# A pre-norm transformer block on one core: queries, keys and values of tiles 4 to 15 in three 512-column chains, logits kept in PSUM

## The chip, the core and the metric

The kernel runs on one core of one Trainium2 chip. The core has a matrix engine (TensorE; in the profile PE, and PEld for its weight loads), a vector engine (VectorE, DVE), a scalar engine (ScalarE, ACT), a general engine (GpSimd, POOL), and SyncE (SP), from which nearly all transfers are issued. Each engine takes its own instructions strictly in order and waits on semaphores for the others. [...] The metric is device microseconds from the first to the last instruction of one execution, as a median of runs.

## The reference: what is computed

x is 2048 rows of 512. The first half of the block is attention, the second a wide layer with a squared ReLU:

```
h   = x + attention(layernorm(x) @ wqkv) @ wo          # 32 heads of 16
out = h + (relu(layernorm(h) @ w1 + b1)**2) @ w2 + b2   # 512 -> 1792 -> 512
```

Attention is local and dilated: row s looks at the eight rows s, s-2, ..., s-14 (those below 0 are masked), with a softmax over these eight for each head. All is float32 in and out.

## The kernel before, in words

The rows are cut into 16 tiles of 128. A tile takes every eighth row or so (`x_v`), so that the eight keys of a query lie in the same partition. All large products are made to float32 accuracy from two parts of each operand, a rounded high part (`hi`, L116, a cast on ACT) and the rest (`lo`, L119, a subtraction on DVE or POOL); `mm3` (L181) sums high by high, low by high and high by low over four blocks of 128, so a product is a chain of 12 matmuls into one PSUM bank.

**Queries, keys, values.** `qkv(t, gp)` makes, for tile t and one of four pairs of head groups `gp`, 128 columns each of queries, keys and values: a chain of 12 matmuls of 384 columns. Tiles 0 to 3 are done pair by pair (16 slots), tiles 4 to 15 in six phases (`first_phase(t0)`) of two tiles and eight chains. ACT copies a chain's bank to the tile `y2` (`evac`, L425), which has two buffers of two chains each; SP stores a full buffer to a DRAM scratch `qkv_d` (`store`, L411), from which SP loads the shifted windows of keys and values (L200) and the queries (L213). `store_halo` (L405) copies a few rows inside that scratch, once for each `gp`.

**Attention** runs on DVE beside the matmuls, as a stream of 32 items of two tiles' worth of one pair `gp`. An item multiplies queries by keys (L276, twice), reduces to logits `lg` (L302, L316), adds the mask (L321, half of the items), takes the maximum (L329), subtracts it (L331); ACT takes the exponential into a PSUM tile `ex` (L335); DVE sums (L298), inverts (L305), scales (L311) and weighs the values (L287, twice); POOL adds the weighed values up to `o` (L346). `lg` lies in SBUF, `ex` in PSUM.

**The order of the work** is written out by a small planner. The program is cut into slots, one to a chain or so; `at(d, ...)` and `after(d, ...)` put a chore at the end of a slot, `after` behind the attention that `pump` adds. `pump` adds attention steps as long as a planned VectorE time (the numbers after `yield`, times `SLOW`) is below the planned TensorE time (the argument of `end_slot`). The numbers only set the order; nothing waits for a clock. The chores of a phase: statistics and normalisation of the next two tiles (`x_stats` on DVE and POOL, `x_norm` on ACT, L151), their transposes (`x_T`, L156, then `hi_T` on ACT and `lo_T` on DVE), loads of their rows (`load_x`, L375), and `weight_job`: load a piece of wo or w1 (L463) into a buffer called `raw`, and five slots later split it into its parts on ACT and POOL.

**The wide layer** takes eight groups s of two tiles. For each of 14 blocks f of the hidden layer, `mlp1` (12 matmuls of 256 columns into one of two banks `mm`), then on ACT relu, square and rounding (`hidden`, L540, L541, L116), POOL's low part `rl`, and three slots later `mlp2` (6 matmuls of 512). During s = 0 the weights w2 are loaded (`load_w2`, L686) three blocks ahead and split on ACT and DVE (`split_w2`). In the same slots the attention output of the next group is transposed (`o_T`), multiplied by wo (`wo_product`) and normalised (`h_norm`). The last two groups are done together as a wide group (512 columns in `mlp1`); `add_b2` (L500, POOL) adds a bias to h, `finish` (L570) adds the result and stores it. One pool of 15 row-sized buffers (`ROWS`) serves xt, xh, xl, raw, h and others in turn.

## Time and profile before

| | |
|---|---|
| median of 3 runs | 528.54 us (527.89 to 528.81) |
| the profiled execution's own time | 529.14 us |
| its span, first to last instruction | 527.3 us |
| TensorE (PE) busy | 519.3 us, 98% |
| weight loads (PEld) busy | 471.3 us, 89% |
| VectorE (DVE) busy | 381.1 us, 72% |
| GpSimd (POOL) busy | 309.9 us, 59% |
| ScalarE (ACT) busy | 251.5 us, 48% |
| granted TensorE clock | 0.998 of full speed |

The profile gives each instruction's start and length, and for an idle stretch of an engine who ended it. Matmuls overlap in the records (a matmul's row is longer than the time to the next one's start), so the cost of a matmul in a stream is read from the starts of the rows, not from its own length. A row "A <- B: total, times, longest" says that A stood idle until B was done.

### The profile page before, as it was taken

The numbers are of one execution on the slowest core, as the hardware profiler recorded it, in microseconds if no ns is written. First come the engines' busy times: TensorE is split into PE (matmuls) and PEld (weight loads), VectorE is DVE, ScalarE is ACT, GpSimd is POOL, SyncE is SP. The second block draws the span as 40 slices with busy tenths as digits, with TensorE's granted clock in tenths as the row PEclk, the third lists the DMA queues.
The fourth block names the chain that finished last, engine by engine and source line by source line (L and its number), as shares of the span: only waits on it lengthen the run. The fifth ranks groups of instructions, "written<-read, shape, count | busy, mean of one in ns | idle before, by whom it ended". The sixth has DMA issues, their size and how long they took to land.

```text
span 527.3 us, 8630 instructions
## 1 busy us (share of the span) xinstructions
PE 519.3 (98%) x3024; PEld 471.3 (89%) x3024; DVE 381.1 (72%) x566; ACT 251.5 (48%) x565; POOL 309.9 (59%) x424
## 2 busy tenths in 40 slices
PE   8999999999999999999999999999999999999997
PEld 7999899999999889988989898898989888888885
DVE  5478999988898799997998899699979324111112
ACT  4623554454347566555626464463636335442421
POOL 4715678778675479686877786776879717000000
PEclk9999999999999999999999999999999999999999
DMA  9568978897678454544544453454435000100002
GB/s 266 175 206 197 277 256 244 254 285 238 183 213 284 132 167 121 173 122 133 180 136 122 131 176 117 133 180 124 126 100 179 8 1 1 40 1 0 2 0 80
DMA packets 70659, 75.93 MB, mean 144 GB/s; under 512 B 6744, under 2 KB 47704, under 8 KB 70616
## 3 DMA queue, kind: packets, MB, share of 16 engines
q1 hardware_dynamic: 69816, 75.00, 47.2%
q8 instruction: 23, 0.38, 0.3%
q10 hardware_dynamic: 800, 0.39, 0.3%
q14 instruction: 20, 0.16, 0.1%
HBM read 58.50 MB, written 16.91 MB: 143 GB/s over the span
## 4 chain that ended last, share of the span: by engine, by line
PE 57%; issue 3%; POOL 3%; ACT 0%; DVE 0%; POOLq 0%; DVEq 0%; ACTq 0%
PE mm L181 25%; PE acc L563 25%; PE wo L181 5%; PE tr L156 2%; POOL rl L119 1%; POOL rs L135 1%; POOL h L500 0%; POOL pr L346 0%; DVE pr L287 0%; POOL rs L137 0%; POOL rs L133 0%; ACT hn L151 0%; DVE h L570 0%; ACT r L540 0%; POOL o L346 0%
## 5 line engine op out<-in xcount | busy, mean ns | idle before, releaser
L346 POOL TENSOR_TENSOR pr<-pr 128x512 f32<-128x512 f32 (+1 forms) x128 | 131.3, 1026 | 37.2 <-DVE pr L287 31.9
L540 ACT ACTIVATE r<-mm,b_sb 128x256 f32<-128x256 f32 (+1 forms) x98 | 49.4, 505 | 120.0 <-PE mm L181 110.2
L119 POOL TENSOR_TENSOR rl<-r,rh 128x256 fp32r<-128x256 f32 x84 | 62.4, 747 | 58.1 <-ACT rh L116 58.1
L287 DVE TENSOR_TENSOR pr<-ex,v 128x1024 f32<-128x1024 f32 x64 | 78.0, 1219 | 5.6 <-POOL o L346 3.1
L276 DVE TENSOR_TENSOR pr<-qp,k 128x1024 f32<-128x1024 f32 x64 | 76.0, 1188 | 5.4 <-ACT qp L220 4.8
L181 PE MATMUL mm<-hh,w_h 128*128 128x256 f32 (+1 forms) x392 | 69.8, 300 | 0.0
L181 PE MATMUL mm<-hl,w_h 128*128 128x256 f32 (+1 forms) x392 | 69.0, 298 | 0.0
L181 PE MATMUL mm<-hh,w_l 128*128 128x256 f32 (+1 forms) x392 | 68.9, 298 | 0.0
L181 PEld LDWEIGHTS mm<-hh,w_h 128*128 128x128 f32 x392 | 59.9, 189 | 6.8 <-ACT r L540 0.2
L425 ACT COPY y<-mm 128x384 f32<-128x384 f32 x64 | 30.3, 481 | 63.1 <-PE mm L181 37.5
L181 PEld LDWEIGHTS mm<-hl,w_h 128*128 128x128 f32 x392 | 56.8, 191 | 2.2
L181 PEld LDWEIGHTS mm<-hh,w_l 128*128 128x128 f32 x392 | 56.7, 191 | 2.2
L563 PE MATMUL acc<-w_h,rh 128*128 128x512 f32 x192 | 58.6, 397 | 0.0
L563 PE MATMUL acc<-w_h,rl 128*128 128x512 f32 x192 | 57.6, 391 | 0.3 <-POOL rl L119 0.3
L563 PE MATMUL acc<-w_l,rh 128*128 128x512 f32 x192 | 57.7, 391 | 0.0
L181 PE MATMUL mm<-wq_h,xh 128*128 128x384 f32 x256 | 56.6, 342 | 0.7 <-ACT xh L116 0.7
L181 PE MATMUL mm<-wq_h,xl 128*128 128x384 f32 x256 | 55.1, 336 | 0.5 <-DVE xl L119 0.5
L181 PE MATMUL mm<-wq_l,xh 128*128 128x384 f32 x256 | 55.2, 336 | 0.0
L119 DVE TENSOR_TENSOR rl<-r,rh 128x512 fp32r<-128x512 f32 x14 | 9.7, 692 | 59.8 <-ACT rh L116 59.8
L181 PEld LDWEIGHTS mm<-wq_h,xl 128*128 128x128 f32 x256 | 45.0, 188 | 1.5 <-DVE xl L119 1.1
L181 PEld LDWEIGHTS mm<-wq_h,xh 128*128 128x128 f32 x256 | 44.2, 188 | 1.8 <-ACT xh L116 1.5
L541 ACT ACTIVATE r<-r 128x256 f32<-128x256 f32 (+1 forms) x98 | 44.0, 448 | 3.1
(76 smaller groups left out, 859.4 us busy)
## 6 DMA issues: line engine op xcount, KB each, us to landing
k<-qkv_d SPq DMA_DIRECT2D x48, 288.0 KB, 2.8
v<-qkv_d SPq DMA_DIRECT2D x48, 288.0 KB, 2.7
qkv_d<-y SPq DMA_DIRECT2D x32, 384.0 KB, 4.1
xt<-in_A_x_dram SPq DMA_DIRECT2D x16, 256.0 KB, 4.3
q<-qkv_d SPq DMA_DIRECT2D x32, 128.0 KB, 3.0
h<-in_A_x_dram SPq DMA_DIRECT2D x16, 256.0 KB, 3.8
out_dram<-h SPq DMA_DIRECT2D x16, 256.0 KB, 2.9
raw<-in_B_w_dram SPq DMA_DIRECT2D x16, 224.0 KB, 4.3
```

Source lines behind the costliest of these rows:

```text
L119: eng.tensor_tensor(out=dst, in0=src, in1=h, op=ALU.subtract)
L135: nc.gpsimd.tensor_tensor(out=rs[:, 0:1], in0=rs[:, 1:2], in1=mhalf, op=ALU.pow)
L156: nc.tensor.transpose(tr[:, k, :], src[:, k * P:(k + 1) * P], ident)
L181: nc.tensor.matmul(ps, l(k), r(k), start=(n == 0), stop=(n == 3 * KB - 1))
L276: nc.vector.tensor_tensor(out=pr.rearrange("p i w h d -> p i w (h d)"), in0=qp[:, j].unsqueeze(2).to_broadcast([P, RI, W, GC]), in1=kwin, ...
L287: nc.vector.tensor_tensor(out=p2, in1=vwin, op=ALU.mult, in0=e1[:, :, :, j * GH:(j + 1) * GH].unsqueeze(4).to_broadcast([P, RI, W, GH, DH]))
L346: nc.gpsimd.tensor_tensor(out=dst, in0=p2[:, :, :w], in1=p2[:, :, w:2 * w], op=ALU.add)
L425: nc.scalar.copy(y[:, :, t % RI * GC:(t % RI + 1) * GC], ps[:, :3 * GP].rearrange("p (j c) -> p j c", j=6))
L540: nc.scalar.activation(r, ps, AF.Relu, bias=b1_sb[:, f:f + 1])
L541: nc.scalar.activation(r, r, AF.Square)
L563: nc.tensor.matmul(acc[j], l[:, j * P:(j + 1) * P], w[f], start=(f == 0 and n < len(js)), stop=(f == FB - 1 and n >= len(terms) - len(js)))
```

## The change

What it does:

- **Three chains of 512 for tiles 4 to 15.** `qkv_of(t, c)` makes all 512 columns of queries (c = 0), keys (1) or values (2) of a tile: 3 chains of 12 matmuls a tile in place of 4. The DRAM scratch is laid out by query/key/value first. `y2` grows to eight groups, a store is 512 KB in place of 384 KB, and attention may start on a group of four tiles only when the value chain of its last pair is stored. For tiles 0 to 3 the chains stay, but each store becomes two, one for each half of the pair.
- **Half-chain slots.** In these phases a slot is half a chain: `mm3` calls back after six matmuls, and chores (transposes too) may be put there. The places of chores are the new tables `XT`, `OT`, `WO`, `HT`, `W2`. `weight_job` still splits five slots after its load, which are now half-chain slots.
- **Logits in PSUM.** One PSUM tile `logits` (the old bank `ex`) of two halves holds an item's logits; mask, maximum, subtraction and exponential work in place.
- **Planned times** of slots and attention steps have other values.
- **Last tile by halves.** The last tile's last six matmuls become twelve of 256 columns in two banks; its other ten-odd blocks are added to h earlier; each half is added and stored by itself, one from SP, one from ACT.
- **Smaller moves.** w2 is loaded two blocks ahead in place of three, the low part of its last block lies in `y2`'s place and not in a row buffer, `ROWS` is 14, `h_norm` of the last group comes a slot earlier, and the four last `add_b2` come together at the start of the wide group.

The diff, cut to its core:

```diff
-ROWS = 15
+ROWS = 14
-SLOW = 1.1, 1.05
+SLOW = 1.08, 1.03
+XT = 9, 11
+OT = 7, 8
+WO = 10, 12
+HT = 20, 22
+W2 = 17, 18
-    qkv_d = dram.tile([2, G // 2, 3, 2, CH + PAD, GC], F32, name="qkv_d")
+    qkv_d = dram.tile([2, 3, G, CH + PAD, GC], F32, name="qkv_d")
...
+        logits = psum.tile([P, 2, RI, W, 2, GH], F32, name="ex")
...
-                lg = att.tile([P, RI, W, 2, GH], F32, name="lg")
+                lg = logits[:, n % 2]
...
-                ex[n] = psum.tile([P, RI, W, 2 * GH], F32, name="ex")
-                yield 0.55
-                nc.scalar.activation(ex[n], lf, AF.Exp, scale=DH ** -0.5)
+                ex[n] = lf
+                yield 0.72
+                nc.scalar.activation(lf, lf, AF.Exp, scale=DH ** -0.5)
...
+        if c is None:
+            for j in range(2):
+                nc.sync.dma_start(chain(e, 2 * gp + j, 0, pos,
+                                        [[R * GC, P], [G * CS, 3], [1, RI * GC]]), y[:, :, j])
+        else:
+            nc.sync.dma_start(chain(e, 0, c, pos, [[R * GC, P], [CS, G], [1, RI * GC]]), y)
...
+    def qkv_of(t, c, mid):
+
+        ps = bank()
+        xh, xl = xT[t]
+        cs = slice(c * D, (c + 1) * D)
+        mm3(ps, lambda k: xh[:, k, :], lambda k: xl[:, k, :],
+            lambda k: wq_h[:, k, cs], lambda k: wq_l[:, k, cs], mid, 3 * KB // 2)
+        at(1, evac, t, 0, c, ps)
...
+        def half(m):
+            end_slot(1.37)
+            chores(m)
+
+        for n in range(6):
+            chores(2 * n)
+            qkv_of(t0 + n % 2, n // 2, lambda: half(2 * n + 1))
+            end_slot(1.37)
...
-                if f + 3 < FB:
-                    load_w2(f + 3)
+                if f + 2 < FB:
+                    load_w2(f + 2)
...
-        after(3, h_norm, s, j)
+        after(2 if s == NS - 1 else 3, h_norm, s, j)
...
-    for j in range(RI):
-        after(0, add_b2, s + 1, j)
+    for j in range(LAST * RI):
+        after(0, add_b2, s + j // RI, j % RI)
...
+    def last_tile(s, j, fs):
+
+
+        u, b, e, i0 = where(NS - 1)
+        h = hs.pop((NS - 1, RI - 1))
+        js = slice(j * P, (j + 1) * P)
+        for c, eng in ((slice(0, D // 2), nc.sync), (slice(D // 2, D), nc.scalar)):
+            ps = psum.tile([P, D // 2], F32, name="half", tag="tr", bufs=2)
+            terms = [(f, l, w) for f in fs for l, w in ((0, w2_h), (1, w2_h), (0, w2_l))]
+            for n, (f, l, w) in enumerate(terms):
+                nc.tensor.matmul(ps, hid[s, f][l][:, js], w[f][:, c], start=(n == 0),
+                                 stop=(n == len(terms) - 1))
+            nc.vector.tensor_tensor(out=h[:, c], in0=ps, in1=h[:, c], op=ALU.add)
+            eng.dma_start(out_v[b, e, i0 + RI - 1, :, c], h[:, c])
```

How the order moves, at three places. A name's number is its buffer; a line number is that of its own kernel.

First TensorE, in the phase of tiles 4 and 5 (xh_563 is tile 4 and xh_594 tile 5 before; 567 and 599 after), around the transposes of the next tile, number 6 (xt_512 before, xt_515 after). Before, the fifth and sixth chain, the transposes, the seventh:

```order
L181 MATMUL mm_708<-wq_h_84,xh_563 128x384 x4
L181 MATMUL mm_708<-wq_h_84,xl_564 128x384 x4
L181 MATMUL mm_708<-wq_l_85,xh_563 128x384 x4
L181 MATMUL mm_735<-wq_h_84,xh_594 128x384 x4
L181 MATMUL mm_735<-wq_h_84,xl_595 128x384 x4
L181 MATMUL mm_735<-wq_l_85,xh_594 128x384 x4
L156 MATMUL tr_768<-ident_80,xt_512 128x128 x4
L181 MATMUL mm_775<-wq_h_84,xh_563 128x384 x4
```

and after, the fifth of six chains, with the transposes in its middle:

```order
L185 MATMUL mm_700<-wq_l_85,xh_599 128x512 x4
L185 MATMUL mm_727<-wq_h_84,xh_567 128x512 x4
L185 MATMUL mm_727<-wq_h_84,xl_568 128x512 x2
L160 MATMUL tr_752<-ident_80,xt_515 128x128 x4
L185 MATMUL mm_727<-wq_h_84,xl_568 128x512 x2
L185 MATMUL mm_727<-wq_l_85,xh_567 128x512 x4
L185 MATMUL mm_773<-wq_h_84,xh_599 128x512 x4
```

The transposes stood behind six chains of 384; now they stand behind four and a half of 512.

Second ScalarE in the same phase: copies of chains (mm) to y2, the normalisation of tile 6 (xt_512, now xt_515) and tile 7 (xt_566, now xt_570), a copy of queries (qp) and the split of wo (wo_h). Before:

```order
L425 COPY y2_90<-mm_614 128x6x64
L425 COPY y2_90<-mm_641 128x6x64
L425 COPY y2_90<-mm_665 128x6x64
L425 COPY y2_90<-mm_690 128x6x64
L151 ACTIVATE xt_512<-xt_512,rs_632 128x512
L220 COPY qp_728<-q_611 128x256
L116 CAST wo_h_86<-raw_635 128x512
L425 COPY y2_90<-mm_708 128x6x64
L151 ACTIVATE xt_566<-xt_566,rs_657 128x512
```

and after:

```order
L442 COPY y2_90<-mm_617 128x8x64
L442 COPY y2_90<-mm_647 128x8x64
L120 CAST wo_h_86<-raw_632 128x512
L442 COPY y2_90<-mm_674 128x8x64
L155 ACTIVATE xt_515<-xt_515,rs_629 128x512
L224 COPY qp_713<-q_614 128x256
L155 ACTIVATE xt_570<-xt_570,rs_657 128x512
L120 CAST wo_h_86<-raw_669 128x512
L442 COPY y2_90<-mm_700 128x8x64
```

Four copies stood ahead of the normalisation of tile 6; now three copies and the first split of wo do.

Third SyncE, where the wide layer begins: loads of w2 (raw2, one for each block f), the last stores of y2, windows of keys and values, and rows of x for h. Before, from the load for f = 2 to that for f = 4:

```order
L686 DMA raw2_1931<-in_B_w2_dram 128x512
L200 DMA v_1936<-qkv_d_77 128x576
L411 DMA qkv_d_77<-y2_90 128x6x128
L200 DMA v_1975<-qkv_d_77 128x576
L200 DMA k_2013<-qkv_d_77 128x576
L213 DMA q_2015<-qkv_d_77 128x2x128
L686 DMA raw2_2037<-in_B_w2_dram 128x512
L478 DMA h_2040<-in_A_x_dram 128x512
L411 DMA qkv_d_77<-y2_90 128x6x128
L686 DMA raw2_2058<-in_B_w2_dram 128x512
```

and after, from the load for f = 1 to that for f = 4:

```order
L737 DMA raw2_1730<-in_B_w2_dram 128x512
L425 DMA qkv_d_77<-y2_90 128x8x128
L204 DMA k_1765<-qkv_d_77 128x576
L204 DMA v_1777<-qkv_d_77 128x576
L737 DMA raw2_1828<-in_B_w2_dram 128x512
L507 DMA h_1831<-in_A_x_dram 128x512
L425 DMA qkv_d_77<-y2_90 128x8x128
L204 DMA v_1837<-qkv_d_77 128x576
L737 DMA raw2_1853<-in_B_w2_dram 128x512
L507 DMA h_1861<-in_A_x_dram 128x512
L737 DMA raw2_1879<-in_B_w2_dram 128x512
```

The load for f = 3 (raw2_2037, now raw2_1853) stood ahead of the last store of y2 and of one load of h; now it stands behind that store and a window of values.

More of the change, by code (lines that the diff above doesn't have):

```diff
@@ L156, in transposes @@
             nc.tensor.transpose(tr[:, k, :], src[:, k * P:(k + 1) * P], ident)
-        now["pe"] += 0.45
+        now["pe"] += 0.44
         return tr
@@ L178, in mm3 @@
         for n, (l, r, k) in enumerate(terms):
-            if mid and n == 2 * KB:
+            if mid and n == at_:
                 mid()
@@ L295, in attention @@
                 pr = dots(0)
[L296 removed]
+                yield 1.22
             if old:
@@ L406, in store_halo, with store @@
                               chain(0, g, 2, PAD, [[0, 2], [0, PAD], [1, GC]]))
-    def store(t, gp, y):
+    def store(t, gp, c, y):
         b, r = divmod(t, 8)
         e, i = divmod(r, 4)
-        nc.sync.dma_start(chain(e, 2 * gp, 0, PAD + CH // 2 * b + i,
-                                [[R * GC, P], [CS, 6], [1, RI * GC]]), y)
+        pos = PAD + CH // 2 * b + i
+        if c is None:
[4 more added lines that the diff above has]
+            nc.sync.dma_start(chain(e, 0, c, pos, [[R * GC, P], [CS, G], [1, RI * GC]]), y)
         if t == 0:
@@ L415, in store, with evac @@
         if i == R - RI:
-            stored.add((t // R, gp))
+            if c is None:
+                stored.add((t // R, gp))
+            elif c == 2:
+                stored.update((t // R, gp) for gp in range(G // 2))
     ys = {}
-    y2 = wpool.tile([P, 2, 6, RI * GC], F32, name="y2", tag="y2")
-    def evac(t, gp, ps):
+    y2 = wpool.tile([P, 2, G, RI * GC], F32, name="y2", tag="y2")
+    def evac(t, gp, c, ps):
+        j = 6 if c is None else G
         if t % RI == 0:
-            ys[gp] = y2[:, nbank[0] // RI % 2]
-        y = ys[gp]
+            ys[gp, c] = y2[:, nbank[0] // RI % 2, :j]
+        y = ys[gp, c]
         nc.scalar.copy(y[:, :, t % RI * GC:(t % RI + 1) * GC],
-                       ps[:, :3 * GP].rearrange("p (j c) -> p j c", j=6))
+                       ps[:, :j * GC].rearrange("p (j c) -> p j c", j=j))
         if t % RI == RI - 1:
-            at(0, store, t - t % RI, gp, ys.pop(gp))
+            if c is None:
+                y = y.rearrange("p (c j) n -> p c j n", c=3)
+            at(0, store, t - t % RI, gp, c, y)
+            del ys[gp, c]
+    def qkv_of(t, c, mid):
[5 more added lines that the diff above has]
+        at(1, evac, t, 0, c, ps)
     def qkv(t, gp, mid=None):
@@ L552, in mlp1, with mlp2 @@
         at(1, hidden, s, f, ps)
-    def mlp2(s, f, acc, js):
+    def mlp2(s, f, acc, js, last=FB - 1):
         rh, rl = hid[s, f]
@@ L564, in mlp2 @@
                              start=(f == 0 and n < len(js)),
-                             stop=(f == FB - 1 and n >= len(terms) - len(js)))
+                             stop=(f == last and n >= len(terms) - len(js)))
     def finish(s, j, a):
@@ L650, in block_kernel, with chores @@
             x_T(n - 10)
-        end_slot(1.95)
+        end_slot(2.09)
     def first_phase(t0):
-        for n in range(8):
-            gp, t = n // 2, t0 + n % 2
+        def chores(m):
             if t0 + 3 < 16:
-                if n in (0, 1):
-                    at(0, x_stats, t0 + 2 + n)
-                if n in (4, 5):
-                    at(0, x_norm, t0 - 2 + n)
-                if n in (6, 7):
-                    x_T(t0 - 4 + n)
-            if t0 + 5 < 16 and n in (4, 6):
-                at(0, load_x, t0 + 2 + n // 2)
-            k = 8 * ((t0 - 12) // 2) + n - 4
-            if k in (10, 11):
-                h_T(0, k - 10)
-                after(0, add_b2, 0, k - 10)
-            qkv(t, gp)
-            if jobs and n % WJ == 0:
-                at(0, weight_job)
-            if k in (0, 1):
-                at(0, load_h, 0, k)
-                o_T(0, k)
-            if k in (3, 4):
-                wo_product(0, k - 3)
-                now["pe"] += 2.6
-            if k in (7, 8, 9):
-                at(0, load_w2, k - 7)
-            end_slot(1.95)
+                if m in (0, 2):
+                    at(0, x_stats, t0 + 2 + m // 2)
+                if m in (6, 7):
+                    at(0, x_norm, t0 - 4 + m)
+                if m in XT:
+                    x_T(t0 + 2 + XT.index(m))
+            if t0 + 5 < 16 and m in (6, 9):
+                at(0, load_x, t0 + 2 + m // 3)
+            if jobs and m % 3 == 0:
+                at(0, weight_job)
+            k = t0 // 2 * 12 - 72 + m
+            if k in OT:
+                at(0, load_h, 0, OT.index(k))
+                o_T(0, OT.index(k))
+            if k in WO:
+                wo_product(0, WO.index(k))
+                now["pe"] += 2.73
+            if k in HT:
+                h_T(0, HT.index(k))
+                after(0, add_b2, 0, HT.index(k))
+            if k in W2:
+                at(0, load_w2, W2.index(k))
+        def half(m):
[5 more added lines that the diff above has]
+            end_slot(1.37)
     def load_w2(f):
@@ L693, in block_kernel @@
     big2_l = wpool.tile([P, 12, D], F32R, name="w2_l", tag="big_l")
-    big2_x = wpool.tile([P, 3, D], F32R, name="w2_x", tag="y2")
+    big2_x = wpool.tile([P, 4, D], F32R, name="w2_x", tag="y2")
     for f in range(12):
         w2_h[f], w2_l[f] = big2_h[:, f, :], big2_l[:, f, :]
-    w2_h[12], w2_l[12], w2_h[13] = [big2_x[:, n, :] for n in range(3)]
-    w2_l[13] = row("w2l", dt=F32R)
+    w2_h[12], w2_l[12], w2_h[13], w2_l[13] = [big2_x[:, n, :] for n in range(4)]
     def split_w2(f):
@@ L736, in block_kernel @@
                 mlp2(s, f - LAG, acc, js)
-                more += 1.3
-            end_slot(1.3 + more)
+                more += 1.39
+            end_slot(1.44 + more)
         for n, f in enumerate(range(FB - LAG, FB)):
@@ L759, in block_kernel @@
         if f >= LAGW:
-            mlp2(s, f - LAGW, acc, js)
+            for j in (js[:-1], js[-1:]) if f == FB - 1 else (js,):
+                mlp2(s, f - LAGW, acc, j, FB - 1 if len(j) > 1 else f - LAGW)
         end_slot(5.4 if f >= LAGW else 2.7)
-    for j in js:
+    h = hs[NS - 1, RI - 1]
+    for j in js[:-1]:
         for f in range(FB - LAGW, FB):
@@ L767, in block_kernel @@
         at(0, finish, s + j // RI, j % RI, acc[j])
+        if j == 1:
+            at(0, nc.vector.tensor_tensor, h, acc[-1], h, ALU.add)
         if j:
             run(due)
-    run(due)
+    last_tile(s, js[-1], range(FB - LAGW, FB))
 _INS = ['A_x', 'A_wqkv', 'A_wo', 'B_w1', 'B_b1', 'B_w2', 'B_b2']
```

32 lines of the change are left out of this document (15 added, 17 removed).

## The prediction, made before the changed kernel was run

> **What bounds it.** I read the page's head first, then who waited for whom, then the matrix engine's starts in order of time, then the engines that its waits name.
>
> ```profile
> PE 519.3 (98%) x3024; PEld 471.3 (89%) x3024; DVE 381.1 (72%) x566; ACT 251.5 (48%) x565; POOL 309.9 (59%) x424
> ```
>
> TensorE is busy for 98%, so time goes only with what its stream needs and the few holes in it. What a matmul costs there is read from starts. Rows of 384-column chains (one row is four matmuls, a chain is three rows) and, from the chain of waits, of 256 and 512 columns:
>
> ```profile
> 18.91 0.85 PE L181 MATMUL mm<-wq_h,xh 128*128 128x384 f32 x4
> 35.55 0.85 PE L181 MATMUL mm<-wq_h,xh 128*128 128x384 f32 x4
> ...
> 214.29 1.43 PE mm L181 x12
> 215.72 1.39 PE acc L563 x6
> ...
> 219.92 2.72 PE wo L181 x12
> ```
>
> From 18.91 to 35.55 lie eight chains: 16.64 / 8 = 2.08 us, 173.3 ns a matmul. At 512 columns it is 2.72 / 12 = 226.7 ns, at 256 it is 119 ns. 128 columns more cost 53.4 ns, so about 13 ns of each matmul do not depend on its width.
>
> The holes, with what ended each at the row's end; by starts they are larger, since a row outlasts its matmul:
>
> ```profile
> 44.68 0.95 PE L181 MATMUL mm<-wq_h,xh 128*128 128x384 f32 x4
> 45.84 0.97 PE L181 MATMUL mm<-wq_h,xl 128*128 128x384 f32 x4 [0.21 <-DVE xl L119]
> ...
> 47.37 0.86 PE L181 MATMUL mm<-wq_h,xh 128*128 128x384 f32 x4
> 48.48 0.96 PE L181 MATMUL mm<-wq_h,xl 128*128 128x384 f32 x4 [0.26 <-DVE xl L119]
> ...
> 57.63 0.86 PE L181 MATMUL mm<-wq_l,xh 128*128 128x384 f32 x4
> 59.49 0.66 PE L156 MATMUL tr<-ident,xt 128*128 128x128 f32 x4 [1.01 <-ACT xt L151]
> ...
> 64.61 0.85 PE L181 MATMUL mm<-wq_h,xh 128*128 128x384 f32 x4
> ```
>
> Four matmuls of 384 take 0.69 us. So 0.47, 0.42 and 1.17 us are lost, all in the phase of tiles 4 and 5, which lasts from 44.68 to 64.61. Two more come later, and the end:
>
> ```profile
> 191.08 0.63 PE L563 MATMUL acc<-w_l,rh 128*128 128x512 f32 x2
> 192.00 0.73 PE L563 MATMUL acc<-w_h,rl 128*128 128x512 f32 x2 [0.29 <-POOL rl L119]
> ...
> 444.39 0.62 PE L563 MATMUL acc<-w_x,rl 128*128 128x512 f32 x2
> 445.23 0.65 PE L156 MATMUL tr<-ident,hn 128*128 128x128 f32 x4 [0.21 <-ACT hn L151]
> ...
> 523.53 0.69 DVE h L570
> ```
>
> Two matmuls of 512 take 0.45 us, so these lose 0.47 (0.55 with a slow restart) and 0.39 us. After the last addition, which ends at 524.22, 3.1 us pass to the span's end at 527.3.
>
> **The change part by part**, against the profiled execution's 529.14 us.
>
> *Chains, tiles 6 to 15.* Ten tiles: 40 chains of 2.08 become 30 of 2.72, 83.2 to 81.6: -1.6 us. Nothing hides it either way. Transposes put into a chain's middle are as many as before. A wait could appear here: `weight_job`'s split comes after five half chains, 6.8 us, not five chains, 10.4 us, and stands in ACT's queue ahead of copies. The loads land in 4.3 us (below), so it costs nothing while SP issues them in time.
>
> [...]
>
> *The phase of tiles 4 and 5.* Its pace is set on ACT by the tile-6 normalisation:
>
> ```profile
> 57.87 0.86 ACT L425 COPY y<-mm 128x384 f32<-128x384 f32 x2 [4.71 <-DMA qkv_d<-y]
> 58.62 0.82 ACT L151 ACTIVATE xt<-xt,rs 128x512 f32<-128x512 f32 x1
> ...
> 52.22 1.19 SPq L405 DMA_DIRECT2D qkv_d<-qkv_d  x2
> 53.51 0.35 SPq L463 DMA_DIRECT2D raw<-in_A_wo_dram  x1
> 53.95 0.38 SPq L411 DMA_DIRECT2D qkv_d<-y  x1
> ...
> raw<-in_A_wo_dram SPq DMA_DIRECT2D x4, 256.0 KB, 3.1
> raw<-in_B_w_dram SPq DMA_DIRECT2D x16, 224.0 KB, 4.3
> ...
> L116 ACT CAST xh<-tr 128x512 fp32r<-128x512 f32 x16 | 9.4, 590 | 5.7 <-PE tr L156 5.7
> ```
>
> Before it, ACT copies two chains into a y2 buffer that becomes free when the store issued at 53.95 lands, just before 57.87. That store is late because SP stood behind the halo copies until 52.22. All this stays. Now one copy, of 512 columns (0.59, as the cast of that size), stands between the landing and the normalisation, not two (0.75): -0.16 us. The wo split is new ahead of it, but its load lands at 53.51 + 3.1 = 56.6 and the split ends by 57.3, before the store lands. The store itself is two issues; each of the three stores in question adds up to 0.4 us on SP, so it lands 0 to 1.2 us later. The transfers ahead of the middle one were still moving when it was issued, so I take 0.3. After the transposes come one and a half chains of 512, not two of 384: 4.08 for 4.16. Sum -0.16 + 0.3 - 0.08, so about 0, with -0.3 and +1.0 as ends. The stream reaches the transposes earlier (4.5 chains of 2.72, 12.2 us, stand ahead of them and not 6 of 2.08, 12.5) and waits longer. So the 0.9 us lost on xl go into the longer wait, and the width gains nothing here.
>
> *Logits in PSUM.* Groups of the same size, in SBUF (first three) and in PSUM:
>
> ```profile
> L331 DVE TENSOR_TENSOR lg<-lg,mx 128x128 f32<-128x128 f32 x32 | 20.2, 632 | 1.1
> L329 DVE TENSOR_REDUCE mx<-lg 128x16 f32<-128x128 f32 x32 | 12.4, 388 | 0.0
> L321 DVE TENSOR_TENSOR lg<-lg,mask 128x128 f32<-128x128 f32 x16 | 8.2, 514 | 0.3
> L311 DVE TENSOR_TENSOR ex<-ex,sm 128x128 f32<-128x128 f32 x32 | 9.1, 285 | 0.0
> L298 DVE TENSOR_REDUCE sm<-ex 128x16 f32<-128x128 f32 x32 | 9.0, 281 | 5.4 <-ACT ex L335 5.4
> ...
> 190.00:264.00 74.00, 73.71 (x469) 66.08 (x468) 69.29 (x103) 43.45 (x105) 59.57 (x77) 1.00 0.48 144
> ```
>
> Subtraction and mask should fall to 285 ns, the maximum to 281: 32 x 0.347 + 16 x 0.229 + 32 x 0.107 = 18 us of DVE. The reductions into PSUM have no row; L311 writes PSUM, L298 SBUF, and they differ by 4 ns, so I add nothing. DVE is not on the path: the gain is worth what it saves TensorE in waits. The window from 190 shows DVE busy for 69.29 of 74 us; POOL's rl at 191 stood behind sums that waited for DVE. With DVE ahead I take -0.4 of these 0.55 (ends 0 and -0.55).
>
> [...]
>
> *The start of the wide group.* The normalisation that TensorE awaited at 445.23 came after two bias additions on POOL, now moved behind it:
>
> ```profile
> 441.75 1.25 POOL h L500
> ...
> 444.36 0.83 ACT hn L151
> ```
>
> One addition alone, 1.25 us, exceeds the hole: -0.4 (ends 0 and -0.4). POOL has nothing to do later that the moved additions could delay.
>
> *The end.* Six matmuls of 512 (1.36) become twelve of 256 (1.43), +0.07. The last addition of 128x512 (0.69) becomes 128x256, and that size has a row:
>
> ```profile
> L119 DVE TENSOR_TENSOR hl<-tr,hh 128x256 fp32r<-128x256 f32 x32 | 12.0, 417 | 24.1 <-ACT hh L116 24.1
> q<-qkv_d SPq DMA_DIRECT2D x32, 128.0 KB, 3.0
> ```
>
> -0.27. A transfer of 128 KB lands in 3.0 us, about the 3.1 that pass now with 256 KB, so nothing more: -0.2 (ends -0.7, if half the bytes save half a microsecond, and +0.2, if ACT issues slower).
>
> *w2 two blocks ahead.* At the start of the wide layer ACT waited for w2 even before:
>
> ```profile
> 167.23 0.62 ACT L116 CAST w_h<-raw 128x512 fp32r<-128x512 f32 x1 [1.16 <-DMA raw<-in_B_w_dram]
> 167.75 0.47 ACT L540 ACTIVATE r<-mm,b_sb 128x256 f32<-128x256 f32 x1
> ...
> 169.64 0.64 PE L181 MATMUL mm<-hh,w_h 128*128 128x256 f32 x4
> ```
>
> That is the part for f = 3. Behind the cast stand relu, square and rounding of the block before, without which `mlp1` gets no bank two blocks later. That relu, at 167.75, ended 1.4 us before the bank was needed at 169.64. The load now stands behind the last store of y2 and a window too: two issues of some 0.4 (the store at 53.95), within the 1.4. I take +0.2; 0 at the low end, the high end is a rival.
>
> Sum: -1.6 + 0 - 0.4 - 0.4 - 0.2 + 0.2 = -2.4, 526.7 of 529.14. The median lies 0.60 below the profiled time: 526.1.
>
> **The rivals.**
> *The wait at tile 6 grows.* Three stores in halves are six issues; if all six fall on the path (+1.2) and the wo split, whose load stands behind the halos too, is not hidden (0.64), the phase loses 1.7 where I have 0: -0.7, 527.8, no change. For it: ACT stood 4.71 us for that store. Against: the splits' loads land first.
> *Every hole closes.* If the store lands early, the phase is six chains of 2.72 and eight transposes (0.66 for four at 59.49, of which a third outlasts them; 0.9 in all), 17.2 us, not 19.93: -2.7, and with -1.6, -0.55, -0.4 and -0.5 it is -5.8, 522.8. Against it: nothing moves the halo copies.
> *Width brings nothing.* The six mlp2 matmuls in 1.39 us are 231.7 ns each, and 4/3 of 173.3 is 231: at that price the chains save 0, -0.8 in all, 527.7. Against it: the wo chains, of just this form, at 226.7. [...]
> *w2 comes late: slower.* SP once stood 6.3 us before a load of w2 until a row buffer was free:
>
> ```profile
> SPq L686 <- PE wo L181: 6.3, 1, 6.3
> ```
>
> With one block less of lead and 14 rows, such a hold at f = 2 to 5 makes the cast 6.3 late; beyond 1.4 TensorE waits, 4.9 us. In place of +0.2: -2.4 - 0.2 + 4.9 = +2.3, 530.8. Past 4.0 us of lateness the gain is gone. Against it: the row pool loses one row but also the low part of w2 that sat in it.
>
> **How the numbers follow.** Forecast 0.63; grown wait 0.12; all holes closed 0.08; width without gain 0.05; late w2 0.12. A difference under 0.2% (1.1 us) can't be told from none: below 527.5 is faster. Forecast and closed holes give 0.71 faster, the grown wait and the gainless width 0.17 the same, late w2 0.12 slower. The forecast's own bounds run from -3.4 (every low end) to about 0, 525.1 to 528.5; I take 524.9 to 528.4, which leaves out most of closed holes and late w2.
>
> **What would show it.** Right: q, k and v chains at 2.72 us; one hole left before 64 us, at tile 6's transposes, of some 2 to 2.5 us, ended by ACT xt, and none on xl; maximum and subtraction at some 285 ns; no wait on rl at 191 and none on hn before the wide group; the last addition at 0.42 us. Wrong: a wait of TensorE on a bank or on rl between 160 and 205 us with ACT behind a load of w2; chains at 2.77; reductions into PSUM far over 1.21 us; new waits on xl or xt in later phases.

## The result, and the profile after

The changed kernel takes 523.85 us (median of 4 runs, 523.36 to 524.87) against 528.44 (528.54 in the first three runs): ratio 0.992, 95% interval 0.9907 to 0.9933. The forecast was 526.1, range 524.9 to 528.4: the direction is right, the size is not, about twice the gain forecast. Measured side by side three more times, the changed kernel took 524.38, 523.28 and 523.73 beside 528.63, 528.06 and 528.70.

The profiled execution took 523.98 us, 5.16 less than that of before, with a span of 522.2. The page's line of engines:

```profile
PE 516.7 (99%) x2886; PEld 453.1 (87%) x2886; DVE 373.3 (71%) x568; ACT 250.9 (48%) x553; POOL 310.3 (59%) x424
```

TensorE's starts at the ends of the stages, first of the kernel before (the one such row that is not shown above), then of the changed one; the last three rows are the end:

```profile
158.82 0.63 PE L181 MATMUL mm<-hh,w_h 128*128 128x256 f32 x4
```

```profile
44.84 1.17 PE L185 MATMUL mm<-wq_h,xh 128*128 128x512 f32 x4
...
56.74 0.61 PE L185 MATMUL mm<-wq_h,xl 128*128 128x512 f32 x2
57.62 0.66 PE L160 MATMUL tr<-ident,xt 128*128 128x128 f32 x4 [0.27 <-ACT xt L155]
...
62.70 1.09 PE L185 MATMUL mm<-wq_h,xh 128*128 128x512 f32 x4
...
155.51 0.64 PE L185 MATMUL mm<-hh,w_h 128*128 128x256 f32 x4
...
440.86 0.60 PE L160 MATMUL tr<-ident,hn 128*128 128x128 f32 x4
...
518.80 0.28 PE L613 MATMUL half<-w_x,rh 128*128 128x256 f32 x1
519.12 0.42 DVE L615 TENSOR_TENSOR h<-half,h 128x256 f32<-128x256 f32 x1 [0.29 <-PE half L613]
519.58 0.35 ACTq L616 DMA_DIRECT2D out_dram<-h  x1
```

From start to start, in us:

| stage | before | after | difference | forecast |
|---|---|---|---|---|
| span's start to tile 4 | 44.68 | 44.84 | +0.16 | 0 |
| tiles 4 and 5 | 19.93 | 17.86 | -2.07 | 0 |
| tiles 6 to 15 (with wo) | 94.21 | 92.81 | -1.40 | -1.6 |
| wide layer, to the last transposes of hn | 286.41 | 285.35 | -1.06 | -0.6 (-0.4 -0.4 +0.2) |
| from there to the span's end | 82.09 | 81.32 | -0.77 | -0.2 |
| sum | | | -5.14 | -2.4 |

In these two executions three quarters of the error lie in one stage, tiles 4 and 5. What is left there is one hole, between the rows at 56.74 and 57.62: two matmuls of 512 take 0.45, so 0.43 us are lost. The waits on xl, rl and hn are gone. The -2.07 is made up of -1.0 on xl, -0.74 at tile 6 (1.17 to 0.43) and -0.3 from the chains themselves (eight of 2.08 became six of 2.72). SyncE and ScalarE in that stage:

```profile
50.28 1.24 SPq L412 DMA_DIRECT2D qkv_d<-qkv_d  x2
...
52.52 0.89 SPq L422 DMA_DIRECT2D qkv_d<-y  x2
```

```profile
56.27 0.59 ACT L442 COPY y<-mm 128x512 f32<-128x512 f32 x1 [0.76 <-DMA qkv_d<-y]
56.75 0.82 ACT L155 ACTIVATE xt<-xt,rs 128x512 f32<-128x512 f32 x1
```

The chain is the one that the prediction described (halo copies, store, its landing, copy, normalisation, transposes), but all of it comes 1.4 to 1.9 us earlier: halo copies 50.28 for 52.22, store 52.52 for 53.95, normalisation 56.75 for 58.62. The groups of VectorE:

```profile
L309 DVE TENSOR_REDUCE ex<-pr 128x64 f32<-128x1024 f32 x32 | 39.2, 1226 | 1.0
L338 DVE TENSOR_TENSOR ex<-ex,mx 128x128 f32<-128x128 f32 x32 | 9.6, 300 | 1.1
L336 DVE TENSOR_REDUCE mx<-ex 128x16 f32<-128x128 f32 x32 | 8.9, 278 | 0.0
L328 DVE TENSOR_TENSOR ex<-ex,mask 128x128 f32<-128x128 f32 x16 | 4.7, 295 | 0.3
```

Subtraction 632 to 300 ns, maximum 388 to 278, mask 514 to 295: as forecast. The reductions into PSUM take 1226 ns each, 18 more than into SBUF before (1208).

### The profile page after: what moved, and what is told of

Read it like the earlier page. It is cut to its first block, busy times and chain, and to the rows that moved or that the text cites. A ratio compares the mean times of both kernels' runs of the same rounds, so it can differ in the third digit from the quotient of the medians.

```text
span 522.2 us, 8355 instructions
## 1 busy us (share of the span) xinstructions
PE 516.7 (99%) x2886; PEld 453.1 (87%) x2886; DVE 373.3 (71%) x568; ACT 250.9 (48%) x553; POOL 310.3 (59%) x424
## 4 chain that ended last, share of the span: by engine, by line
PE 96%; DMA 2%; SPq 0%; issue 0%; ACT 0%; DVE 0%; ACTq 0%
PE mm L185 53%; PE acc L592 29%; PE wo L185 8%; PE tr L160 4%; DMA qkv_d<-y 2%; DMA xt<-in_A_x_dram 1%; PE half L613 0%; SPq L412 0%; ACT xh L120 0%; ACT xt L155 0%; DVE st L131 0%; DVE xt L151 0%; DVE h L615 0%; SPq L382 0%; SPq L422 0%
## 5 line engine op out<-in xcount | busy, mean ns | idle before, releaser
L185 PE MATMUL mm<-wq_h,xl 128*128 128x512 f32 (+1 forms) x208 | 55.2, 378 | 0.0
L185 PE MATMUL mm<-wq_h,xh 128*128 128x512 f32 (+1 forms) x208 | 53.2, 377 | 0.7 <-ACT xh L120 0.7
L185 PE MATMUL mm<-wq_l,xh 128*128 128x512 f32 (+1 forms) x208 | 52.7, 375 | 0.0
L442 ACT COPY y<-mm 128x512 f32<-128x512 f32 (+1 forms) x52 | 28.6, 556 | 45.2 <-PE mm L185 24.6
L120 ACT CAST rh<-r 128x256 fp32r<-128x256 f32 (+1 forms) x98 | 43.0, 438 | 3.1
L185 PEld LDWEIGHTS mm<-wq_h,xh 128*128 128x128 f32 x208 | 37.8, 188 | 7.2 <-ACT xh L120 1.8
```

What stands on the lines that cost most here:

```text
L120: nc.scalar.copy(dst, src)
L185: nc.tensor.matmul(ps, l(k), r(k), start=(n == 0), stop=(n == 3 * KB - 1))
L442: nc.scalar.copy(y[:, :, t % RI * GC:(t % RI + 1) * GC], ps[:, :j * GC].rearrange("p (j c) -> p j c", j=j))
```

## Experiments

What is open: why tiles 4 and 5 lost 2 us. The candidates: **H**, halves of the first stores land earlier; **D**, a lighter VectorE; **L**, the new layout of the scratch; **W**, the chains of 512 with the new places of copies and normalisations. Later came **C** and **S**, named below. Runs of one kernel differ by 2 us and more (before: 526.93 to 531.57), so each experiment is read twice: by its median, and by the places in its profile. The table has the second, worked out from the starts of SyncE's, VectorE's and TensorE's rows. "First store": from its issue to the start of the first halo copy, which waits for it (with halves, for the first half alone); "x rows": when VectorE, waiting for a load of x rows, goes on; "halo": start of the last two halo copies; then the time lost on xl in the first chains of tiles 4 and 5, at tile 6's transposes, and the time of tiles 4 to 15 together.

| kernel | first store | x rows | halo | xl | tile 6 | tiles 4-15 | median |
|---|---|---|---|---|---|---|---|
| before | 3.82 | 32.27 | 52.22 | 1.01 | 1.17 | 114.14 | 528.4 |
| halves (b_halves) | 3.08 | 31.55 | 49.62 | 0.11 | 0 | 112.84 | 528.39 |
| PSUM (b_psum) | 3.39 | 31.48 | 50.86 | 0.48 | 0.35 | 112.75 | 527.88 |
| end (b_ends) | 4.17 | 32.62 | 52.21 | 1.45 | 0.81 | 114.20 | 527.99 |
| these three (b_three) | 2.81 | 30.77 | 49.84 | 0 | 0.17 | 112.54 | 526.53 |
| earlier normalisation (b_norm) | 4.01 | 32.25 | 51.80 | 1.05 | 0 | 113.60 | 527.94 |
| halo copies later (b_halo) | 3.55 | 32.20 | moved | 1.08 | 0 | 113.29 | 528.10 |
| changed | 2.92 | 31.15 | 50.28 | 0 | 0.43 | 110.67 | 523.85 |
| again (a_again) | 3.37 | 31.55 | 50.82 | 0 | 1.24 | 111.48 | 524.38 |
| third (a_third) | 3.24 | 30.46 | 49.50 | 0 | 0 | 110.21 | 523.28 |
| fourth (a_fourth) | 3.31 | 30.90 | 49.84 | 0 | <0.1 | 110.26 | 523.73 |
| whole stores (a_whole2) | 3.99 | 32.43 | 51.43 | 0.26 | 0.65 | 111.20 | 524.77 |
| logits in SBUF (a_sbuf) | 3.34 | 31.06 | 50.32 | 0 | 0.69 | 110.94 | 524.83 |
| both of these (a_ws) | 4.28 | 32.28 | 51.51 | 0.11 | 0.91 | 111.36 | 525.20 |
| earlier normalisation (a_norm) | 3.02 | 30.22 | 48.83 | 0 | 0 | 110.19 | 523.31 |
| the same (a_norm_b) | 3.52 | 32.01 | 51.02 | 0 | 0 | 110.46 | 523.39 |
| halo copies later (a_halo) | 3.70 | 31.99 | moved | 0 | 0 | 110.30 | 523.34 |
| both moves (a_both) | 3.35 | 31.05 | moved | 0 | 0 | 110.22 | 523.39 |

What "x rows" decides is the loss on xl. In the kernel before, VectorE stands still until the load of x rows lands and then works without a gap up to the first of the two xl; the same rows of the changed kernel follow:

```profile
32.27 0.69 DVE L127 BATCH_NORM_STATS2 st<-xt 128x6 f32<-128x512 f32 x1 [3.05 <-DMA xt<-in_A_x_dram]
...
45.11 0.68 DVE L119 TENSOR_TENSOR xl<-tr,xh 128x512 fp32r<-128x512 f32 x1
```

```profile
31.15 0.69 DVE L131 BATCH_NORM_STATS2 st<-xt 128x6 f32<-128x512 f32 x1 [2.25 <-DMA xt<-in_A_x_dram]
...
44.15 0.68 DVE L123 TENSOR_TENSOR xl<-tr,xh 128x512 fp32r<-128x512 f32 x1
```

From the one to the other pass 12.8 to 13.0 us in every profile, 12.8 with the logits in SBUF and 13.0 with them in PSUM. So a lighter VectorE does not bring xl earlier here; an earlier load does.

**One part of the change added to the kernel before.** Halves (the changed store for tiles 0 to 3, in the old layout; shortened):

```diff
+        pos = PAD + CH // 2 * b + i
+        if t < R:
+            y = y.rearrange("p (c j) n -> p c j n", c=3)
+            for j in range(2):
+                nc.sync.dma_start(chain(e, 2 * gp + j, 0, pos,
+                                        [[R * GC, P], [2 * CS, 3], [1, RI * GC]]), y[:, :, j])
...
```

> The kernel before, with one thing changed: each store of tiles 0 to 3 is two transfers of 192 KB in place of one of 384 KB. Theory H (the halves land earlier than the whole store, and all that waits for a store moves up): the first halo copy goes from 18.83 to about 18.1 us, the halo copies at 52.22 to about 50.5, the two losses on xl (0.9 us) vanish and the wait at tile 6 shrinks from 1.17 to 0.5-1; 1.4 to 1.9 us faster than before, 526.5 to 527.0. Rival D (it is the lighter VectorE that moved the phase) and rival L (the new layout of the DRAM scratch did): halo copies stay at 18.8 and 52.2, the phase of tiles 4 and 5 at 19.9 us, no change in time, or 0.2 us slower for eight issues more.

Measured 528.39, ratio 1.0002 (0.9991 to 1.0013). In its profile the halo copies come early, and the stage is short; but the loss moves on to tile 7's transposes:

```profile
18.24 1.34 SPq L405 DMA_DIRECT2D qkv_d<-qkv_d  x2
...
49.62 1.24 SPq L405 DMA_DIRECT2D qkv_d<-qkv_d  x2
```

```profile
59.40 0.86 PE L181 MATMUL mm<-wq_l,xh 128*128 128x384 f32 x4
60.45 0.66 PE L156 MATMUL tr<-ident,xt 128*128 128x128 f32 x4 [0.20 <-ACT xt L151]
...
63.03 0.86 PE L181 MATMUL mm<-wq_h,xh 128*128 128x384 f32 x4
63.91 0.96 PE L181 MATMUL mm<-wq_h,xl 128*128 128x384 f32 x4
```

0.36 us are lost at 60.45, because in chains of 384 the next copy stands behind the next store, and 0.2 on an xl at 63.91. The times show no gain from halves alone. The early halo copies came in the old layout, so they do not need the new one (L); no run changes the layout alone. Logits in PSUM, as the change has them (shortened):

```diff
+        logits = psum.tile([P, 2, RI, W, 2, GH], F32, name="ex")
-                lg = att.tile([P, RI, W, 2, GH], F32, name="lg")
+                lg = logits[:, n % 2]
-                ex[n] = psum.tile([P, RI, W, 2 * GH], F32, name="ex")
-                nc.scalar.activation(ex[n], lf, AF.Exp, scale=DH ** -0.5)
+                ex[n] = lf
+                nc.scalar.activation(lf, lf, AF.Exp, scale=DH ** -0.5)
```

> The kernel before with the logits kept in PSUM, planned times as before. Theory H: the phase of tiles 4 and 5 stays at 19.9 us (within 0.3), since the first store is late before attention has begun; only the wait on rl at 191 us (0.55 with its restart) shrinks; 0.3 to 0.6 us faster, about 528.0. Rival D: the halo copies at 52.22 come 1.5 us or more earlier and the phase loses 1 to 2 us; 526 to 527. Subtraction 632, maximum 388 and mask 514 ns all fall to 280-300 in either case.

527.88, ratio 0.9991 (0.9979 to 1.0003). The wait on rl is gone (the wide layer to hn loses 0.50 us of start to start), as H and the forecast had it. The halo copies came 1.4 us earlier too, but the first store landed 0.4 earlier already, before any logit is computed: part of that is the execution's own. The end, with `last_tile` and the `mlp2` calls of the change:

```diff
-        after(3, h_norm, s, j)
+        after(2 if s == NS - 1 else 3, h_norm, s, j)
-                after(0, add_b2, s + 1, f - FB + RI)
-    for j in range(RI):
-        after(0, add_b2, s + 1, j)
+    for j in range(LAST * RI):
+        after(0, add_b2, s + j // RI, j % RI)
-    for j in js:
+    for j in js[:-1]:
...
-    run(due)
+    last_tile(s, js[-1], range(FB - LAGW, FB))
```

> The kernel before with the last tile by halves, the four bias additions together at the start of the wide group and the last normalisation a slot earlier. By the two traces: the hole of 0.39 us before the wide group goes, and from the start of the last matmul to the span's end pass 3.4 us and not 4.26; 1.2 us faster, about 527.2. By the prediction's terms: 0.4 and 0.2, 0.6 us faster, about 527.8.

527.99, ratio 0.9994 (0.9983 to 1.0005). The profile shows the two fixed gains (from the last transposes of hn to the end 81.5 for 82.09 us, and the hole of 0.38 ahead of them gone), 1.0 us together; the interval reaches to -0.9. From the last matmul's start to the span's end pass 3.56 us, not the 3.4 expected. All three together:

> The kernel before with halves of stores, logits in PSUM and the changed end together, and without the chains of 512 and their slots. If the chains are worth the 1.2 us of TensorE that the rows of tiles 6 to 15 show and nothing else, this is 1.2 us slower than the changed kernel, 525.1. By theory W it is 2.2 to 2.8 slower, since the new places in the phase of tiles 4 and 5 are lacking too: 526.1 to 526.7. If the three do not add up beyond what they gave alone (0.04, 0.55 and 0.44 us), 527.4.

526.53, ratio 0.9966 (0.9949 to 0.9983). That lies where W put it, but not for W's reason. Parts of a difference that do not vary between executions (the wide layer up to hn and the stretch behind it agree within 0.02 us in four profiles of the changed kernel) can be read from the stages: against the changed kernel 1.40 us in tiles 6 to 15, 0.3 in tiles 4 and 5 (eight chains of 2.08 for six of 2.72) and 0.3 in the wide layer and the end, 2.0 of the 2.15 by medians. So by medians the two kernels have about the same holes. Against the kernel before, 0.5 (rl) and 1.0 (end) of the 2.10 are fixed and 0.6 are holes.

**One part taken out of the changed kernel.** Whole stores (the scratch then laid out head group first, so that six pieces lie at one stride):

```diff
-        block = (e * 3 + c) * G + g
+        block = (e * G + g) * 3 + c
-            for j in range(2):
-                nc.sync.dma_start(chain(e, 2 * gp + j, 0, pos, ...), y[:, :, j])
+            nc.sync.dma_start(chain(e, 2 * gp, 0, pos, [[R * GC, P], [CS, 6], [1, RI * GC]]), y)
```

> The changed kernel with the stores of tiles 0 to 3 whole again (384 KB each); for that the DRAM scratch is laid out by head group first and query/key/value second, a layout that neither kernel has. Theory H: first halo copies back at 18.8, those of the phase of tiles 4 and 5 at 52 or later; that phase loses 1.5 to 2.3 us at tile 6; 525.4 to 526.2. Rivals D and L: as the changed kernel, 523.9 within 0.4.

525.30 (523.64 to 526.24, 4 runs). Its profile can't be used for the stage: TensorE's first chain began 1.5 us late (9.71 for 8.19), its matmuls then started 320 ns apart until 12.4 us (some 175 in the kernel before), tile 4 began 2.8 us late, and the stores had that much time. So again, with two others:

> The changed kernel with the stores of tiles 0 to 3 whole (and the scratch laid out by head group first), again. Theory H (halves land earlier): 1.0 to 1.6 us slower than the changed kernel. Theory W (the new places of copies, normalisation and stores in the phase of tiles 4 and 5 took the holes away, whatever the size of the stores before it) and theory D (the lighter VectorE did): within 0.3 of it.

Logits back in SBUF:

```diff
-                lg = logits[:, n % 2]
+                lg = att.tile([P, RI, W, 2, GH], F32, name="lg")
-                ex[n] = lf
+                ex[n] = logits[:, n % 2].rearrange("p i w j h -> p i w (j h)")
-                nc.scalar.activation(lf, lf, AF.Exp, scale=DH ** -0.5)
+                nc.scalar.activation(ex[n], lf, AF.Exp, scale=DH ** -0.5)
```

> The changed kernel with the logits back in SBUF (the exponential writes PSUM), planned times as they are. Theory D: the holes of the phase of tiles 4 and 5 come back, 1 to 2 us, and the wait on rl at 190 us too, 0.5: 525.4 to 526.4. Theories H and W: only the wait on rl comes back, and VectorE behind the plan by 18 us may bring others after 120 us: 524.3 to 525.

> The changed kernel once more, beside the three others of this call, since runs of one kernel differ by up to a microsecond or two: 523.9 within 0.3, and in its profile a hole at tile 6 of 0 to 0.8 us, none on xl, rl or hn.

Whole stores 524.77 (ratio 0.9937, 0.9915 to 0.9959), logits in SBUF 524.83 (0.9931, 0.9912 to 0.995), changed 524.38 (0.9916, 0.9898 to 0.9935): no two of them can be told apart. Logits in SBUF bring no hole of 1 to 2 us, so D is out as the main cause, and for xl the 12.8 to 13.0 us above say the same. What logits in SBUF cost is a wait in the wide layer, on another tile than rl:

```profile
203.77 0.83 PE L185 MATMUL mm<-hl,w_h 128*128 128x256 f32 x4 [0.34 <-DVE hl L123]
```

The changed kernel's own hole was 1.24 us this time, ended as ever:

```profile
58.25 0.66 PE L160 MATMUL tr<-ident,xt 128*128 128x128 f32 x4 [1.08 <-ACT xt L155]
```

Both parts out (these two diffs together), against the kernel before with the changed end:

> The changed kernel without two of its parts: stores of tiles 0 to 3 whole, logits in SBUF. Against the kernel before with the changed end alone (528.0) it differs by the chains of 512, their slots and the planned times. If the chains bring the 1.2 us of TensorE and nothing else: 526.8. By theory W (their new places also take 1 us of holes out of the phase of tiles 4 and 5): 525.6 to 526.0. Against the changed kernel: 0.5 for the wait on rl, and 0.4 to 1.0 for whole stores.

> The changed kernel, a third time, to compare the others of this call with: 524.0 within 0.4; a hole at tile 6 of 0.3 to 1.3 us.

525.20 (0.9953, 0.9939 to 0.9967) beside 523.28 (0.9916, 0.9903 to 0.9928), below what either theory gave, since both counted too little as fixed. Its profile speaks for W: the chains with their new places took the losses on xl (1.01 to 0.11) and left 0.91 at tile 6:

```profile
58.24 0.66 PE L160 MATMUL tr<-ident,xt 128*128 128x128 f32 x4 [0.74 <-ACT xt L155]
```

Its median speaks against W: it is 2.86 below that of the kernel before, measured beside it, and the stages' fixed parts make 2.8 of it (1.4, 0.3 and 1.1 behind the chains). Of the 1.92 us to the changed kernel, 0.72 are the wide layer (that much longer to hn in the profile, with the wait on hl), 1.15 are holes in tiles 4 to 15.

**Where the hole at tile 6 comes from.** Theory C: only ScalarE's order carries the store's landing to TensorE. In both kernels the normalisations come two slots earlier (shown for the changed one):

```diff
-                if m in (6, 7):
-                    at(0, x_norm, t0 - 4 + m)
+                if m in (4, 5):
+                    at(0, x_norm, t0 - 2 + m)
```

> The kernel before with the normalisations of the next two tiles two slots earlier, ahead of the third copy to y2. Theory C: the hole at tile 6 (1.17 us in the profile before) goes, the two waits on xl stay; 0.7 to 1.2 us faster than before, 527.3 to 527.8. Rival: within 0.3 of before, because the pace is the stores' own and the wait turns up at the next tile's copy or on a PSUM bank.

> The changed kernel with the normalisations of the next two tiles two half-chain slots earlier, ahead of the third copy to y2 on ScalarE. Theory C (the hole at tile 6 is the landing of the last store of tiles 0 to 3, carried to TensorE only by ScalarE's order: copy first, normalisation behind it): the hole of 0.4 to 1.3 us at tile 6 is gone in the profile and nothing takes its place; 0.4 to 0.8 us faster than the changed kernel, 523.2 to 523.6. Rival: the normalisation waits for its statistics instead, or the casts of xh come late behind the copy: no gain, 524.0 to 524.6.

The kernel before took 527.94 (0.9995, 0.9984 to 1.0005). The hole at tile 6 is gone, since the normalisation now runs at 52.63 and not at 58.62, ahead of the copy that waits for the landing:

```profile
52.63 0.83 ACT L151 ACTIVATE xt<-xt,rs 128x512 f32<-128x512 f32 x1
57.32 0.48 ACT L425 COPY y<-mm 128x384 f32<-128x384 f32 x1 [3.85 <-DMA qkv_d<-y]
```

TensorE and VectorE further on:

```profile
83.29 0.86 PE L181 MATMUL mm<-wq_h,xh 128*128 128x384 f32 x4
84.22 0.97 PE L181 MATMUL mm<-wq_h,xl 128*128 128x384 f32 x4
...
82.40 1.17 DVE L331 TENSOR_TENSOR lg<-lg,mx 128x128 f32<-128x128 f32 x1
83.49 0.68 DVE L119 TENSOR_TENSOR xl<-tr,xh 128x512 fp32r<-128x512 f32 x1
```

The lower rows show a loss in a new place, 0.24 us on the xl of a later tile. No store is in it: VectorE, without a gap, has a subtraction of 1.17 us ahead of that xl. Another 0.2 us are lost on an xl at 64.17. So tiles 4 to 15 take 0.54 us less, not 1.17. C holds for the place, and the forecast of 0.7 to 1.2 us failed. The changed kernel with the same move took 523.31; its sister beside it happened to have no hole either, so this pair says nothing of the gain. Theory S: what makes the store late is SyncE's order. The store issued at 53.95 had its data since the copy that ended at 47.68; it stood behind halo copies that wait for the store before it. They go one slot later, behind that store:

```diff
-            at(2, store_halo, gp)
+            at(3 if gp else 2, store_halo, gp)
```

> The kernel before with the halo copies of head groups 2 to 8 one slot later, so that on SyncE they stand behind the next store of y2 and not ahead of it; nothing else is moved. Theory S (the pace of the phase of tiles 4 and 5 is set by stores that are ready and stand behind halo copies: the one issued at 53.95 had its data at 47.68): that store goes out by 48.5, the hole at tile 6 and the waits on xl go, the phase takes 17.7 to 18.0 us and not 19.93; 1.5 to 2.2 us faster than before, 526.3 to 526.9. Rival: the landing itself is the limit (the queue is full), the store goes earlier and lands as late; within 0.5 of before.

> The changed kernel with the same move of the halo copies. Theory S: no hole at tile 6 whatever the chip; 523.2 to 523.4 with a spread of 0.3, as its runs without a hole had. Rival: as the changed kernel beside it.

> The changed kernel with the normalisations two half-chain slots earlier, again. Where the changed kernel beside it has a hole at tile 6, this one has none: 523.2 to 523.5, and a spread of 0.3.

> The changed kernel, to compare the others with: between 523.2 (no hole) and 524.5 (a hole of 1.2 us at tile 6).

The kernel before, SyncE, ScalarE and TensorE:

```profile
48.13 0.44 SPq L411 DMA_DIRECT2D qkv_d<-y  x1
51.62 1.19 SPq L405 DMA_DIRECT2D qkv_d<-qkv_d  x2
```

```profile
54.72 0.81 ACT L151 ACTIVATE xt<-xt,rs 128x512 f32<-128x512 f32 x1
```

```profile
45.77 0.97 PE L181 MATMUL mm<-wq_h,xl 128*128 128x384 f32 x4 [0.27 <-DVE xl L119]
...
48.41 0.96 PE L181 MATMUL mm<-wq_h,xl 128*128 128x384 f32 x4 [0.27 <-DVE xl L119]
```

The store goes out at 48.13, the normalisation runs 3.9 us earlier, and tile 6 loses nothing: S holds for this hole. The two waits on xl stay, which S had gone too: the x rows land as late as before (32.20 for 32.27 in the table), and this move leaves what stands ahead of their load as it was. 528.10 beside 528.70, ratio 0.9993 (0.998 to 1.0005), 1 us less than S forecast. The changed kernel: 523.34 with the halo copies later (523.29 to 523.52), 523.39 with the earlier normalisation (523.21 to 523.82), 523.73 without either (523.24 to 524.62). Last, both moves together, and both halves of the last tile stored from SyncE:

```diff
-        for c, eng in ((slice(0, D // 2), nc.sync), (slice(D // 2, D), nc.scalar)):
+        for c, eng in ((slice(0, D // 2), nc.sync), (slice(D // 2, D), nc.sync)):
```

> The changed kernel with the halo copies behind the next store and the normalisations two half-chain slots earlier, both. Theories C and S: no hole in the phase of tiles 4 and 5, 523.2 to 523.5, spread 0.3 or less, 0.3 below the median of the changed kernel's 18 runs (523.7).

> The changed kernel with both halves of the last tile stored from SyncE. If the shorter landing is the half size: from the last matmul's start to the span's end 3.4 us, as with ScalarE's queue. If it is the queue: 3.6 us or more.

Both: 523.39 (523.29 to 524.33, 6 runs), no better than one alone, and one run of 524.33 whose cause was not seen. The changed kernel reaches the same floor with and without these moves, about 523.3 (lowest runs 523.18 to 523.36; 523.66 in a_again). The 12 runs with one of the moves lie between 523.18 and 523.82; of 18 runs of the changed kernel as it stands 7 lie above 523.82. So a move is worth a few tenths at most, by taking away the runs with a hole; by medians it can't be told from the changed kernel. Both halves from SyncE (524.1 in its one run, with 0.74 us lost at tile 6): from the last matmul's start to the span's end 3.36 us, as with ScalarE's queue (3.38), and 4.28 before: the queue makes no difference.

## Why the prediction was wrong

**Chains, tiles 6 to 15.** Forecast -1.6, measured -1.40. The price by rows holds (226.7 ns forecast): 60 matmuls of the changed kernel, one piece of its chain of waits, take 227.5 ns each:

```profile
61.48 13.65 PE mm L185 x60
```

**Tiles 4 and 5.** Forecast 0 (-0.3 to +1.0), measured -2.07 in the profiles: the step that failed. The prediction found the chain (halo copies until 52.22, store, landing, copy, normalisation), and b_halo and b_norm show that it is the cause of the hole at tile 6. What failed is the sentence "All this stays", and the +0.3 put on the store for being two issues.

The chain did not stay, because what waits for a store of tiles 0 to 3 now waits for one half. The data as a whole are there no earlier: by the semaphores in the traces a whole first store landed 3.34 to 4.23 us after its issue (seven profiles, without a_whole's; mean 3.84), and the second of two halves 3.32 to 4.43 us after the first was issued (twelve, a_sp's among them; mean 3.79). But the first of the two halo copies needs only the first half. It started 3.39 to 4.28 us after the store when whole (mean 3.89) and 2.81 to 3.70 in halves (mean 3.26). In the changed kernel it starts at 18.12, the second half lands at 18.63, and the second copy starts at 18.87; before, the store lands at 18.78 and the copies start at 18.83 and 19.57. The next issues on SyncE move up, and the next landings with them, so the first 0.6 us grow: the last halo copies came at 50.9 to 52.2 (mean 51.7) with whole stores and at 48.8 to 51.0 (mean 50.05) with halves. The +0.3 was 0: the store that tile 6 waits for landed 3.82 us after its issue before (53.95 to 57.77) and 3.65 after (52.52 to 56.17, both halves).

That xl would no longer be waited for was right, and the table shows why twice over. With halves the x rows land earlier (mean 31.14 in twelve profiles, 32.22 in seven with whole stores), since their load stands on SyncE behind windows that wait for stores (the first window waits 2.1 us for a store before and 1.1 after, and goes out at 22.82 and 21.83; the loads follow at 25.14 and 24.15). And chains of 512 need xl later, four matmuls into the chain, 0.91 us for 0.69: with x rows at 32.0 to 32.4, chains of 384 lose 1.0 to 1.1 us (before, b_norm, b_halo) and those of 512 lose 0 to 0.26 (a_whole2, a_ws, a_norm_b, a_halo). But the waiting that the prediction moved to tile 6 ("some 2 to 2.5 us") was 0 to 1.24 in the seven profiles of the table that keep the changed order there.

The profile that the sum was made against probably had more of these holes than most: its own time is 0.7 us above the median of all runs of that kernel (528.5). The prediction took 0.60 off the answer, as if that surplus stayed after the change. It seems to have sat in the very waits that the change removes: the profiled executions differ by 5.16 us, the medians measured side by side by 4.25 to 4.97. Of that, 3.5 are fixed by the stages (1.40, 0.3 in tiles 4 and 5, 1.06, 0.77), so in the medians the change took away 0.7 to 1.4 us of holes in tiles 4 and 5; in the profiles it was 1.8. The forecast was then short by two errors of one size: 1.1 in the fixed parts (2.4 for 3.5) and about as much in the holes. (The low ends of its terms add up to -3.55 and not -3.4, 525.0; its range begins at 524.9 either way.) In the changed kernel the own times of its four profiles less their hole at tile 6 are 523.55, 523.40, 523.29 and about 523.5: the hole makes nearly all of their spread.

How much each part of the change gained by closing holes is **not settled**. By one profile of each: W 1.1 us (before to a_ws), halves and PSUM the next 0.7 (a_ws to the mean of the changed kernel's four). Medians: W 0.1 (a_ws), halves and PSUM together 0.6 (b_three), neither of them alone anything. The medians' intervals are 0.7 to 0.9 us to either side, and how much the profiles would scatter is not known. Shown are the places, a store's landing passed on by SyncE's and ScalarE's order at tile 6 and the load of x rows at xl, and that a single move closes one place (b_halves, b_norm, b_halo) and leaves or opens another.

**Logits in PSUM.** Durations as forecast, the wait on rl gone, 0.50 us in b_psum for the 0.4 taken. VectorE's busy time fell by 7.8 us (9.2 in b_psum), not by 18: in b_psum the durations added up fell by 15.7, since other rows grew (in b_three's profile, with the logits in PSUM too, the reductions take 1228 and 1222 ns for 1208 and 1206), and a sum of durations counts overlapping rows twice (before, a row of 1.18 us starts at 146.80 and the next at 147.90).

**Start of the wide group, w2.** The wait on hn went as forecast (0.38 us). TensorE waits for nothing between 160 and 205 us: w2 two blocks ahead cost nothing where +0.2 was put. Together with rl the wide layer up to hn gained 1.06 for 0.6.

**The end.** Forecast -0.2 (ends -0.7 and +0.2), measured -0.77: a mis-sized term. The addition gave the 0.27; what follows it gave most of the rest. From the end of the last addition to the span's end 3.10 us passed before (524.22 to 527.32) and 2.64 after (519.54 to 522.18). The end by halves explains 0.27 of this 0.46: b_ends and b_three, with halves at the end and chains of 384, still take 2.82 and 2.83. Every kernel with the chains of 512 takes 2.62 to 2.65, and where those 0.18 us come from no run shows. The prediction took the price of 128 KB from the loads of q, 3.0, another kind of transfer, with windows on the same queue.

**The rivals.** "Every hole closes" (522.8, given 0.08) is what happened in the runs without a hole, 523.3; the result lies nearer to it than to the forecast. Its reason against, that nothing moves the halo copies, is the step that failed. Width without gain, a grown wait and a late w2 did not occur.

## What to carry to other kernels

When a stage's pace is a loop of transfers (store, landing, the next issue behind it), ask of each edit whether it changes a landing, or how much of a transfer each waiter needs, and let the price be open to both sides: "all this stays" was an assumption that no row carried. If the profiled execution is slower than the median, as here by 0.7 us, its surplus may sit in the very waits that vary, so it can't be carried through as a constant. Moving the one late thing ahead on its queue closed its hole here (1.17 us at tile 6 before, 0 in b_norm and b_halo), but while the next waits stood, on xl, the medians showed no gain (ratios 0.9995 and 0.9993).
